# Moves, loads and sums of a fused attention, expert and GLU kernel in another order

## The chip, the cores and the metric

The kernel runs on one core of one Trainium2 chip. The metric is device time in microseconds (us), the median of several executions of the whole program. The program computes in fp32 throughout, with most products written as three fp32r products of high and low parts.

## The reference

Three parts follow one another. Attention: every query attends only to the keys that fall into its bucket of a random projection. Then each token goes to the one of eight experts with the largest logit and is weighted by its gate. Last comes RMS normalisation and a gated linear unit (GLU).

```python
# q, k, v: (2, 8, 768, 64); proj: (64, 6)
q_bits = einsum('bhsd,dk->bhsk', q, proj) > 0        # k_bits likewise
q_bucket = sum(q_bits * 2 ** arange(6), -1)
mask = q_bucket[:, :, :, None] == k_bucket[:, :, None, :]
scores = where(mask, q @ k^T / 8, -1e9)
attn = exp(scores - max(scores)); attn /= sum(attn) + 1e-9
x = (attn @ v) as (1536 tokens, 512)
# experts: w_gate (512, 8), w1 (8, 512, 1024), w2 (8, 1024, 512)
logits = x @ w_gate; e = argmax(logits); gate = softmax(logits)[e]
x = gate * (max(x @ w1[e], 0) @ w2[e])
# GLU: w_gate, w_val (512, 1536), w_out (1536, 512)
xn = x / sqrt(mean(x * x) + 1e-6) * rms_g
g = xn @ w_gate
out = (g * sigmoid(g) * (xn @ w_val)) @ w_out
```

## The kernel before

**Engines and queues.** The order of the work is written out by hand (`manual_schedule`): each engine takes its instructions in the order in which the program emits them, and nearly all DMAs are issued by SP's queue, in that order too. A DMA in that queue that waits for its source holds back all that come after it.

**Attention.** There are 16 heads (two batches of eight), with 768 tokens in six tiles of 128. The loop at line 931 runs over 96 units, one for each head and query tile; `n` is the head of unit `u` and `t` its tile. In each unit a string of letters (`ORDER`, in the last four units `LATE`) fixes the order of the steps: scores of the unit after next ("S"), maxima, exponentials of the next unit, transposes of the exponentials, the product with v ("A", `av`), the handing back of a finished group of three tiles (`keep`, `give_back`), and one step of a filler ("f", `fill_next`). A filler is a generator; the one that matters here is `prep_head(n)`, in eight steps: PE transposes k and q of the head (line 514), ACT and DVE write their scaled high and low parts `kqh` and `kql` (lines 516, 517), PE multiplies with the projection (lines 544 to 546), and DVE and POOL make of the signs the feature rows `ft` (lines 551, 552). In between, `moves()` (line 508) places the parts with six DMAs from SBUF to SBUF into qA, qB, kA and kB, the operands of the scores (lines 563, 564), and two more DMAs (lines 554, 555) bring `ft` there. `kqh`, `kql` and `ft` have one buffer each, so the next head's are written only when these moves have read them. `ML` says for which heads the moves go out already with the second cast (heads below ML) and not behind the first projection.

`load_head(n)` issues the loads of k, q and (from head 2 on) v. Before the loop the program emits, in this order: the loads of heads 0 and 1, the preparation of head 0, four steps of head 1's preparation, the loads of v of heads 0 and 1 and of the gate weights `wd`, the splitting of v of head 0 by POOL (`split_v`, lines 479 and 480), the loads of head 2 and of the RMS weights `rg`, the first scores, and the other four steps of head 1. The preparation of head 2 is put in at the end of unit 2, so its first step, the transposes, comes at the end of unit 3, just ahead of the scores of unit 6, the first of head 1.

`fill_windows(e)` writes the padding value into the 256 rows of expert e's window of the DRAM buffer `xs`, by two DMAs of 257 KB; it runs at the third and sixth unit of heads 1 to 4, two experts a head. The tokens are scattered over it later.

**Handover to the experts.** Each group of three tiles is handed back by products with an identity that has the gate weights beside it (line 667), so that the tokens by features and the head's share of the eight logits come out together in PSUM. ACT copies them to SBUF as `tb` (line 680), POOL scales the logits by the inverse sum and adds them to `LG`, and scales the features into `X` (lines 693 to 696). The last group (g = 31) comes as three single tiles with a copy each (line 685), and DVE scales and adds its logits. Then `route` chooses the expert (lines 726 to 736), PE counts ranks (line 753), and DVE makes a one-hot `hot` for each of the last three tiles (line 802). The first expert's window is not read back from DRAM alone: it is summed in PSUM (`xacc`) from products of `hot` with the last three tiles (`add_hot`, line 873) and from the window loaded as `base` (`add_base`, line 842: two products with the identity for each of four chunks). While PE waits for the routing, it runs warm-up matmuls (lines 385 and 1023). A branch (line 1044) on the number of overflowing tokens, which every engine loads from `total` (line 1042), jumps over a part that is not run with these inputs.

**Experts.** For each of eight experts: four blocks f of the first product (lines 1222 to 1224, 24 matmuls each), then four of the second (lines 1251 to 1253). The weights come in pieces through a ring of buffers and are split by ACT and DVE. `finish_rows` gates the result, normalises it and scatters it to DRAM (`yd`); it is a generator, and `next(done)` takes one of its steps after each block of the next expert's first product. Its third step holds the reciprocal, both scalings (line 205) and both scatters, and the load of window e + 3 follows it. `fill_pe` takes one step of a list of fillers on PE, such as the transposes of the next window (line 1180).

**GLU.** `flip_y` transposes the twelve tiles of results (line 1141) that `load_y` brings from `yd` (line 1130). Three tiles are loaded after the first block of the last expert, the others one by one as the three buffers come free (`YB`). The flips start after the fourth block of the last expert's first product; five run there, three in the first `glu` and four in the first `project`.

## Time and profile before

| | us |
|---|---|
| median of three runs | 735.92 (735.87 to 736.73) |
| profiled execution | 735.27 |
| its span, first to last instruction | 733.6 |
| attention, up to the warm-up at the handover | 0 to 256 |
| first product of the first expert | 264.7 |
| first flip of the results | 429.2 |
| last matmul | 726.3 |

The profile is of one execution. PE is the matmul engine (PEld its weight loads), DVE the vector engine, ACT the scalar engine, POOL GpSimd and SP the engine that issues DMAs. Times in a timeline are counted from the start of the span. What stands in brackets is how long the engine was idle before an instruction, and which event ended that by the profile; where an instruction waits for several things, the profile names the one whose event came last, and it can be wrong.

### The profile page before, as it was taken

How to read it: one execution, taken by the hardware profiler on the slowest of the kernel's cores; microseconds unless marked ns; L12 is line 12 of the kernel's file. 1: busy time of each engine (PE TensorE's matmuls, PEld its weight loads, DVE VectorE, ACT ScalarE, POOL GpSimd, SP SyncE). 2: the span in 40 equal slices, each digit the busy share in tenths (PEclk: the TensorE clock that was granted, in tenths of full speed). 3: DMA queues.
4: the chain of work that ended last, by engine and by line, in shares of the span. 5: the costliest groups of instructions: out<-in, count | busy, mean ns of one | idle time of the engine just before them, and what ended most of it. 6: DMA issues, size and time to landing. Idle time of an engine off the chain costs nothing.

```text
span 733.6 us, 12489 instructions
## 1 busy us (share of the span) xinstructions
PE 717.4 (98%) x4451; PEld 651.7 (89%) x4452; DVE 577.8 (79%) x1095; ACT 402.9 (55%) x805; POOL 225.6 (31%) x405
## 2 busy tenths in 40 slices
PE   8899999999999999999999999999999999999996
PEld 7798999999999889999999988888888888888885
DVE  6899999999999757787688777756777778778533
ACT  5798998998998735667665555533211222212210
POOL 5143344446635520213022313211211212211124
PEclk9999999999999999999999999999999999999999
DMA  7699856556742147677788674221221121200013
GB/s 182 163 254 263 213 152 154 139 147 173 190 109 70 45 146 246 197 222 246 249 264 265 218 250 150 97 87 58 61 84 58 57 87 59 86 29 1 0 58 115
DMA packets 80546, 103.44 MB, mean 141 GB/s; under 512 B 31799, under 2 KB 50231, under 8 KB 80480
## 3 DMA queue, kind: packets, MB, share of 16 engines
q1 hardware_dynamic: 76480, 92.95, 44.4%
q0 software_dynamic: 3200, 9.46, 3.5%
q8 instruction: 36, 0.59, 0.4%
q10 hardware_dynamic: 800, 0.20, 0.1%
q14 instruction: 30, 0.25, 0.1%
HBM read 69.53 MB, written 14.72 MB: 115 GB/s over the span
## 4 chain that ended last, share of the span: by engine, by line
PE 56%; issue 2%; POOL 2%; ACT 1%; DVE 1%; DMA 1%; SPq 0%; POOLq 0%; DVEq 0%
PE pg L1292 4%; PE pv L1293 4%; PE pg L1293 4%; PE pg L1291 4%; PE pv L1291 4%; PE pv L1292 4%; PE ph L1222 4%; PE ph L1223 4%; PE ph L1224 4%; PE py L1251 3%; PE py L1253 3%; PE py L1252 3%; PE z L1319 3%; PE z L1317 3%; PE z L1318 3%
## 5 line engine op out<-in xcount | busy, mean ns | idle before, releaser
L330 POOL TENSOR_TENSOR wa<-wa,hi 128x512 f32<-128x512 f32 x36 | 58.4, 1623 | 235.4 <-ACT hi L326 203.6
L326 ACT CAST hi<-wa 128x512 fp32r<-128x512 f32 x36 | 22.4, 621 | 151.3 <-DVE wa L324 147.2
L582 ACT ACTIVATE P<-S,negm 128x768 f32<-128x768 f32 x96 | 95.8, 998 | 10.5 <-DVE negm L573 6.4
L611 DVE TENSOR_TENSOR ptl<-T,pth 128x384 fp32r<-128x384 f32 x192 | 97.3, 547 | 1.5 <-ACT pth L610 0.8
L568 DVE TENSOR_REDUCE neg<-S 128x1 f32<-128x768 f32 x96 | 90.8, 946 | 3.6 <-PE S L564 2.9
L610 ACT CAST pth<-T 128x384 fp32r<-128x384 f32 x192 | 83.3, 488 | 3.6 <-PE T L601 2.9
L601 PE MATMUL T<-ident,P 128*128 128x128 f32 x576 | 81.8, 275 | 1.0 <-DVE ptl L611 0.5
L601 PEld LDWEIGHTS T<-ident,P 128*128 128x128 f32 x576 | 67.5, 141 | 7.8 <-DVE ptl L611 4.2
L285 DVE TENSOR_TENSOR lo<-raw,hi 128x1024 fp32r<-128x1024 f32 x58 | 68.7, 1216 | 4.6 <-ACT hi L284 4.6
L284 ACT CAST hi<-raw 128x1024 fp32r<-128x1024 f32 x58 | 60.2, 1055 | 21.0 <-DMA raw<-in_moe_w_dram 20.6
L563 PE MATMUL S<-kA,qA 76*128 76x384 f32 x192 | 66.2, 345 | 3.8 <-ACT kqh L516 1.8
L564 PE MATMUL S<-kB,qB 128*128 128x384 f32 x192 | 63.1, 329 | 0.4 <-DMA qB<-kql 0.4
L1222 PE MATMUL ph<-xTh,hi 128*128 128x256 f32 x224 | 62.6, 279 | 0.0
L1223 PE MATMUL ph<-xTl,hi 128*128 128x256 f32 x224 | 61.6, 275 | 0.0
L1224 PE MATMUL ph<-xTh,lo 128*128 128x256 f32 x224 | 61.6, 275 | 0.0
L633 PE MATMUL O<-ptl,vst 128*64 128x384 f32 (+1 forms) x198 | 59.8, 332 | 0.0
L1317 PE MATMUL z<-hi,hi 128*128 128x512 f32 x144 | 54.9, 381 | 0.0
L1291 PE MATMUL pg<-gxh,hi 128*128 128x512 f32 x144 | 54.7, 380 | 0.0
L1291 PE MATMUL pv<-gxh,hi 128*128 128x512 f32 x144 | 54.7, 380 | 0.0
L1292 PE MATMUL pg<-gxl,hi 128*128 128x512 f32 x144 | 54.7, 380 | 0.0
L1293 PE MATMUL pg<-gxh,lo 128*128 128x512 f32 x144 | 54.6, 379 | 0.0
L1292 PE MATMUL pv<-gxl,hi 128*128 128x512 f32 x144 | 54.6, 379 | 0.0
(236 smaller groups left out, 1911.8 us busy)
## 6 DMA issues: line engine op xcount, KB each, us to landing
raw<-in_moe_w_dram SPq DMA_DIRECT2D x64, 512.0 KB
raw<-in_moe_w_gate_dram SPq DMA_DIRECT2D x12, 512.0 KB
raw<-in_moe_w_val_dram SPq DMA_DIRECT2D x12, 512.0 KB
raw<-in_moe_w_out_dram SPq DMA_DIRECT2D x12, 512.0 KB
xs<-fill SPq DMA_DIRECT2D x16, 257.0 KB
xw<-xs SPq DMA_DIRECT2D x7, 514.0 KB
yt<-yd SPq DMA_DIRECT2D x12, 256.5 KB
qA<-kqh SPq DMA_DIRECT2D x16, 192.0 KB
```

The source lines that it names most:

```text
L568: nc.vector.tensor_reduce(neg[u % 4][:, 1:2], St[u][:, :, 0:HW], AX.XY, ALU.max, negate=True)
L582: nc.scalar.activation(p_, St.pop(u)[:, :, 0:HW], AF.Exp, bias=nm[:, 1:2], scale=nm[:, 0:1], accum_out=sums[n][:, t:t + 1])
L601: nc.tensor.transpose(w[:, c * P:(c + 1) * P], p_[:, j, c * P:(c + 1) * P], ident)
L610: nc.scalar.copy(hi[:, 3 * j:3 * j + 3, cs], wv)
L611: nc.vector.tensor_tensor(lo[:, 3 * j:3 * j + 3, cs], wv, hi[:, 3 * j:3 * j + 3, cs].bitcast(F32), ALU.subtract)
L1222: nc.tensor.matmul(ph[:, s_], wh[:, c, fs], turns(xh[:, c]), start=c == 0, stop=False)
L1223: nc.tensor.matmul(ph[:, s_], wh[:, c, fs], turns(xl[:, c]), start=False, stop=False)
L1224: nc.tensor.matmul(ph[:, s_], wl[:, c, fs], turns(xh[:, c]), start=False, stop=c == KC - 1)
L1291: nc.tensor.matmul(ps_, wh[:, c, fs], turns(xTh[b][:, c]), start=c == 0, stop=False)
L1292: nc.tensor.matmul(ps_, wh[:, c, fs], turns(xTl[b][:, c]), start=False, stop=False)
L1293: nc.tensor.matmul(ps_, wl[:, c, fs], turns(xTh[b][:, c]), start=False, stop=c == KC - 1)
L1317: nc.tensor.matmul(z, hi[:, s_, ts_], turns(oh_[:, s_]), start=s_ == 0, stop=False)
```

## The change

The moves of head 1 go out with its second cast (ML = 2), ahead of the loads of v and `wd`. The loads of head 2 follow the last four steps of head 1, and the RMS weights are loaded in head 10. The fills of the windows run in heads 6 to 9 instead of 1 to 4 (FN = 6). The single tiles of the last group write their logits and features straight from PSUM, and those of the group before it take their logits from PSUM by DVE. The two single tiles after the first share one buffer of another pool. The sums with the identity become transposes that accumulate. The register load for the branch stands ahead of the last sums. `finish_rows` has a further step before each scaling, and `next(done)` is called in the second product too. Five tiles of results are loaded at once, two of them into a window buffer; the flips start one block earlier, and their places in `glu` and `project` change.

```diff
-ML = 1
+ML = 2
+FN = 6
+    YX = 2
@@ finish_rows
         for j in range(J):
+            yield
             nc.vector.scalar_tensor_tensor(y[:, j, 0:DM], y[:, j, 0:DM], st[:, 6, j:j + 1], rg, ALU.mult, ALU.mult)
@@ keep
-                if t0 == 1:
-                    o = ld.tile([P, T, 2 * D], F32, tag="kq", name="osbl")[:, 0]
+                if tn == 1 and t0 > 0:
+                    if t0 == 1:
+                        spare.append(ld.tile([P, T, 2 * D], F32, tag="kq", name="osbl"))
+                    o = spare[-1][:, t0]
@@ give_back, single tiles
-                if t0 == 0:
-                    spare.append(sp.tile([P, 3, PE], F32, tag="tb", name=f"tb{g}"))
-                tb = spare[1]
-                nc.scalar.copy(tb[:, t0], w[:, 0:PE])
+                ls = LG[b][:, 3 * j + t0]
+                r = rinv[n][:, 1, 3 * j + t0:3 * j + t0 + 1]
+                nc.vector.scalar_tensor_tensor(ls, w[:, D:PE], r, ls, ALU.mult, ALU.add)
+                nc.scalar.activation(X[b, j][:, t0, h * D:(h + 1) * D], w[:, 0:D], AF.Copy, scale=r)
                 if t0 < 2:
                     return
@@ give_back, groups of three
-            eng = nc.vector if n == NH - 1 and j == 1 else nc.gpsimd
+                lv, eng = tb[:, :, D:PE], nc.gpsimd
+                if g == 2 * NH - 2:
+                    lv, eng = w[:, 0:3 * PE].rearrange("p (t a) -> p t a", a=PE)[:, :, D:PE], nc.vector
@@ add_base
-                nc.tensor.matmul(xacc[c][:, j * P:(j + 1) * P], base[0][:, j, cs], ident, start=False, stop=j == 1)
+                nc.tensor.matmul(xacc[c][:, j * P:(j + 1) * P], base[0][:, j, cs], ident, start=False, stop=j == 1,
+                                 is_transpose=True)
@@ before the loop
         split_v(0)
         cgen = constants()
-        load_head(2)
-        nc.sync.dma_start(rg, moe2_rms_g.partition_broadcast(P))
 ...
         for i in range(WARM[6]):
             next(fills[0])
+        load_head(2)
@@ in the loop
-            if t in (2, 5) and n > 0 and 2 * (n - 1) + t // 3 < E:
-                fill_windows(2 * (n - 1) + t // 3)
+            if t in (2, 5) and 0 <= 2 * (n - FN) + t // 3 < E:
+                fill_windows(2 * (n - FN) + t // 3)
+            if u == 10 * T:
+                nc.sync.dma_start(rg, moe2_rms_g.partition_broadcast(P))
@@ handover
         add_hot(1, range(KC))
+        any_over = nc.values_load(total[0:1, 0:1], min_val=0, max_val=N)
         for c in range(KC):
 ...
-    any_over = nc.values_load(total[0:1, 0:1], min_val=0, max_val=N)
@@ flip_y
-            if tt + YB < end:
+            if tt >= YX and tt + YB < end:
                 load_y(tt + YB)
@@ experts
-                    for tt in range(YB):
-                        load_y(tt)
-                if e == E - 1 and f == NF - 1:
+                    early = mp.tile([P, 2, XC], F32, tag="xw", name="ytx", bufs=3)
+                    for tt in range(YX + YB):
+                        load_y(tt, early[:, tt, 0:DM + 1] if tt < YX else None)
+                if e == E - 1 and f == 2:
                     fillers.append(flips)
@@ second product of an expert
                 parts.pop(i)
+                next(done, None)
                 fill_pe()
@@ glu and project
-        steps = 3
+        steps = 2
 ...
+                    if p_ == 0 and b == 1 and s_ == 1:
+                        next(flips)
 ...
-                if p_ + b == 0:
+                if p_ + b == 0 and i % 2:
                     next(flips)
```

## Rows read from the trace of the kernel before

**Rows 1.** The page: busy time, share of the span, instructions

```profile
PE 717.4 (98%) x4451; PEld 651.7 (89%) x4452; DVE 577.8 (79%) x1095; ACT 402.9 (55%) x805; POOL 225.6 (31%) x405
```

**Rows 2.** PE's waits: waited for, us in total, times, longest

```profile
PE S L563 <- ACT kqh L516: 1.8, 1, 1.8
...
PE S L563 <- DMA kA<-ft: 1.1, 1, 1.1
...
PE f L1141 <- DMA yt<-yd: 0.9, 1, 0.9
PE wk L753 <- DVE oh L735: 0.7, 1, 0.7
...
PE ph L1222 <- PEq L1044: 0.4, 1, 0.4
```

**Rows 3.** PE's timeline at head 1's first scores: start, duration, instruction, idle before

```profile
22.13 0.49 PE L514 MATMUL wf<-evens,kq 128*128 128x128 f32 x3
24.43 0.40 PE L563 MATMUL S<-kA,qA 76*128 76x384 f32 x1 [1.81 <-ACT kqh L516]
```

**Rows 4.** Timeline of SP's queue at the start

```profile
7.89 1.12 SPq L361 DMA_DIRECT2D v<-in_v_dram  x2
...
17.16 0.67 SPq L508 DMA_DIRECT2D qB<-kqh  x1
...
18.94 0.75 SPq L555 DMA_DIRECT2D kA<-ft  x1
```

**Rows 5.** Timeline of DVE at the start

```profile
10.56 1.14 DVE L517 SCALAR_TENSOR_TENSOR kql<-wf,scv,kqh 128x384 fp32r<-128x384 f32 x2 [1.29 <-DMA qB<-kql]
```

**Rows 6.** Timeline of POOL at the start

```profile
11.02 0.52 POOL L479 TENSOR_SCALAR vst<-v 128x384 fp32r<-128x384 f32 x1 [2.17 <-DMA v<-in_v_dram]
11.62 1.02 POOL L480 TENSOR_TENSOR vst<-v,vst 128x384 fp32r<-128x384 f32 x1
14.43 1.08 POOL L552 TENSOR_SCALAR ft<-ft 12x384 fp32r<-12x384 f32 x2 [1.79 <-DVE ft L551]
```

**Rows 7.** PE's timeline: its last matmul, and warm-up matmuls at the start

```profile
726.31 0.38 PE L1319 MATMUL z<-hi,lo 128*128 128x512 f32 x1
...
1.41 2.31 PE L385 MATMUL warm<-ones 128*128 128x128 bf16 x20 [1.41 <-DVE ones L372]
...
5.16 1.06 PE L385 MATMUL warm<-ones 128*128 128x128 bf16 x8
...
9.32 0.61 PE L385 MATMUL warm<-ones 128*128 128x128 bf16 x8
```

**Rows 8.** Windows: length, busy PE, PEld, DVE, ACT, POOL, clock, DMA share, GB/s

```profile
730.00:731.00 1.00, 0.00 (x0) 0.00 (x0) 0.00 (x0) 0.00 (x0) 0.00 (x0) 0.53 0.46 176
```

**Rows 9.** Windows of 20 us in attention, same columns

```profile
60.00:80.00 20.00, 18.94 (x137) 17.67 (x137) 18.80 (x38) 17.01 (x38) 8.52 (x20) 1.00 0.95 246
...
120.00:140.00 20.00, 20.00 (x144) 18.55 (x144) 19.65 (x43) 17.79 (x40) 9.92 (x22) 1.00 0.52 125
```

**Rows 10.** Timeline of DVE at the handover to the experts

```profile
257.10 0.18 DVE L726 TENSOR_REDUCE rst<-LG 128x3 f32<-128x24 f32 x1
```

**Rows 11.** PE's timeline at the handover

```profile
251.75 0.84 PE L601 MATMUL T<-ident,P 128*128 128x128 f32 x6
...
256.03 1.50 PE L385 MATMUL warm<-ones 128*128 128x128 bf16 x24
...
261.73 0.60 PE L842 MATMUL xacc<-ident,xw 128*128 128x128 f32 x4
262.09 0.48 PE L873 MATMUL xacc<-hot,ftx 128*128 128x256 f32 x2
```

**Rows 12.** The chain that ended last, at the last expert: start, us, what

```profile
433.05 6.14 DMA yt<-yd
```

**Rows 13.** PE's timeline in the last expert: its first matmul, the first flip

```profile
418.49 0.27 PE L1222 MATMUL ph<-xTh,hi 128*128 128x256 f32 x1
...
429.21 0.60 PE L1141 MATMUL f<-ident,yt 128*128 128x128 f32 x4
```

More of the change, by code (lines that the diff above doesn't have):

```diff
@@ L681, in give_back @@
             else:
-                if t0 == 0:
-                    spare.append(sp.tile([P, 3, PE], F32, tag="tb", name=f"tb{g}"))
-                tb = spare[1]
-                nc.scalar.copy(tb[:, t0], w[:, 0:PE])
+                ls = LG[b][:, 3 * j + t0]
+                r = rinv[n][:, 1, 3 * j + t0:3 * j + t0 + 1]
+                nc.vector.scalar_tensor_tensor(ls, w[:, D:PE], r, ls, ALU.mult, ALU.add)
+                nc.scalar.activation(X[b, j][:, t0, h * D:(h + 1) * D], w[:, 0:D], AF.Copy, scale=r)
                 if t0 < 2:
                     return
-            lv = tb[:, :, D:PE]
             scale = rinv[n][:, 1, 3 * j:3 * j + 3].unsqueeze(2)
-            lg = sp.tile([P, 3, E], F32, tag="lg", name=f"lg{g}")
-            eng = nc.vector if n == NH - 1 and j == 1 else nc.gpsimd
-            ls = LG[b][:, 3 * j:3 * j + 3]
-            eng.tensor_tensor(ls if h == 0 else lg, lv, scale.to_broadcast([P, 3, E]), ALU.mult)
-            if h > 0:
-                eng.tensor_tensor(ls, lg, ls, ALU.add)
-            nc.gpsimd.tensor_tensor(X[b, j][:, :, h * D:(h + 1) * D], tb[:, :, 0:D], scale.to_broadcast([P, 3, D]),
-                                    ALU.mult)
+            if tn == 3:
+                lg = sp.tile([P, 3, E], F32, tag="lg", name=f"lg{g}")
+                ls = LG[b][:, 3 * j:3 * j + 3]
+                lv, eng = tb[:, :, D:PE], nc.gpsimd
+                if g == 2 * NH - 2:
+                    lv, eng = w[:, 0:3 * PE].rearrange("p (t a) -> p t a", a=PE)[:, :, D:PE], nc.vector
+                eng.tensor_tensor(ls if h == 0 else lg, lv, scale.to_broadcast([P, 3, E]), ALU.mult)
+                if h > 0:
+                    eng.tensor_tensor(ls, lg, ls, ALU.add)
+                nc.gpsimd.tensor_tensor(X[b, j][:, :, h * D:(h + 1) * D], tb[:, :, 0:D], scale.to_broadcast([P, 3, D]),
+                                        ALU.mult)
             if h == H - 1 and (b == B - 1 or j == 1):
@@ L1126, in lsh_attention_moe_glu, with load_y @@
     yt = {}
-    def load_y(tt):
-        t = gx.tile([P, DM + 1], F32, tag="yt", name=f"yt{tt}", bufs=YB)
+    def load_y(tt, t=None):
+        if t is None:
+            t = gx.tile([P, DM + 1], F32, tag="yt", name=f"yt{tt}", bufs=YB)
         ins = nc.sync.dma_start(t, yd[tt * P:(tt + 1) * P, :]).ins
```

## The prediction

> **What bounds the kernel now.** I read the page first: TensorE is busy for 98% of the span [rows 1], so the time is PE's work plus the little that PE idles. The second view is therefore the list of PE's waits. It is short: 1.8 us at the scores of head 1, 1.1 at the scores of head 4, 0.7 and 0.4 where attention hands over to the experts, 0.9 where the last expert hands over to the GLU [rows 2]. No more than about 5 us can be gained there, and the change works at each of these places. Third, for each place, the timelines of the engines that release it.
>
> One label misleads. The scores of head 1 start at 24.43 and are put down to ACT's cast kqh [rows 2, 3]. They don't read that cast (it is of head 2). They read qA and kA of head 1, whose last piece (kA<-ft) SP issues at 18.94 [rows 4]; a DMA that is 5.5 us from issue to use, behind everything queued before it, explains the time better. So the start is a chain through SP's queue, and that queue is what the change reorders. Of the rows at 22.13 and 24.43 the reader is to see this: PE takes its instructions in order, the flips of head 2 (wf, line 514) stand just ahead of those scores, and had no wait, since kq of head 2 had been loaded long before.
>
> **Part by part. First, the start.** SP's order becomes: three moves of head 0, six moves of head 1, v of heads 0 and 1, the gate weights, the two ft moves of head 1, and only then k, q, v of head 2. Now v of head 0 is issued at 7.89, ahead of the moves [rows 4]; the six moves go later. Who then waits for whom:
> - Moves 2 to 6 of head 1 read kql, which DVE finishes at 10.56 + 1.14 = 11.70 [rows 5]; the step that writes it doesn't move. Five issues at 0.67 each, the row of the last move [rows 4]: v of head 0 goes out at 11.70 + 3.35 = 15.05 instead of 7.89.
> - From its issue to POOL's use, v took 11.02 - 7.89 = 3.1 us with three moves ahead on the rings [rows 4, 6]. With six ahead it is more; the crowded case is the 5.5 us of kA<-ft. Bounds 3.1 and 5.5. I take 4.3, since k, q and v of head 2 and the RMS weights no longer stand in front: POOL can split v at 19.35.
> - POOL's queue is in order, and the scaling of ft stands behind that split. Split 0.60 + 1.02, ft 1.08 [rows 6]: ft is ready at 22.05 (now 15.5).
> - SP then issues the two ft moves, 2 x 0.8 [rows 4], then k of head 2 (0.67) and q at 24.3. At the 3.1 us of v, q lands at 27.4.
> - PE reaches the flips of head 2 at 22.13 as now (the split of v is in time for the first output product, or nearly), and stands there until 27.4. Now the scores follow the flips after 24.43 - 1.81 - 22.13 = 0.5 us [rows 3], so they start at 27.9, and not at 24.43: **3.5 us lost**. Bounds by v's landing: 2.3 and 4.7. What was meant to go, the 1.8 us, is inside this: the moves are early, but they were not what ended last; ft and kq of head 2 are.
>
> Behind the waiting ft moves in SP's queue stand the loads of heads 2 and 3. Head 3 is wanted a head later, so only head 2 counts.
>
> **The clock** is a second charge on the same stall. PE's last matmul ends at 726.31 + 0.38 = 726.7, and the window 730 to 731 has a mean granted clock of 0.53 [rows 7, 8]. So the clock left its upper level (2.4 GHz) for the lower (1.2) at about 730.06, when PE had been idle for 3.4 us. The stall here is 27.4 - 22.1 = 5.3 us. The way back shows at the start: 20 matmuls of 128 columns from 1.41 took 2.31 us, and the eight at 5.16 still took 1.06, against 0.61 for the eight at 9.32 [rows 7]. So until about 6.2, nearly 5 us after the first matmul, the lower level held, and half of such a stretch, 2.4 us, is lost. Bounds 0 and 2.5; I take **2.2 us**. The Trainium skill, in "TensorE: Matmul & The Clock Gate", section "HAM oscillation — how this bites in real kernels", speaks against the change here: a DMA wait between bursts of matmuls sends the clock to its lower level and the next burst starts cold. By that rule the charge comes with the stall. The end of this trace agrees: the clock fell when PE stood idle.
>
> **Fills and RMS weights later.** Sixteen fills of 257 KB leave heads 1 to 4 for heads 6 to 9. From 60 to 80 us the DMA engines are busy for 0.95 of the time at 246 GB/s [rows 9], and that is where head 4's scores wait 1.1 us for kA<-ft [rows 2]. Without the fills that wait goes: 1.1 us gained. Where the fills go, 120 to 140 us, the share is 0.52 at 125 GB/s [rows 9]; four fills of 257 KB in a head of about 15 us (16 heads in some 240 us) add some 70 GB/s, and no wait of PE stands there now. I cost them at nothing. If this cover is gone, the price is one wait like the present one, 1.1 us a head.
>
> **Last logits from PSUM.** ACT's copies of the last tiles and DVE's product and sum fall away from the path to the routing's first reduction at 257.10 [rows 10]; one DVE operation on PSUM a tile replaces them, and the ACT copy of the third tile no longer waits for a buffer. From the end of PE's products (256.0, where the warm-up matmuls start [rows 11]) to 257.10 there is 1.1 us; I leave 0.4 of it for the one operation. That gives 0.7, which is also the wait that PE has [rows 2]; more can't be had, as the warm-up matmuls end at 256.03 + 1.50 = 257.53.
>
> **Sums by transposes.** Each of four chunks has two products with the identity, which PE holds as four records in 262.09 - 261.73 = 0.36 us [rows 11]. A transpose is one record (six for six flips [rows 11]) and not two. Half is saved: 4 x 0.18 = 0.7. But what ends last behind it is the branch, on which PE waits 0.4 [rows 2]; its register load moves ahead of the last sums, so a part goes too. And the first of these sums needs a window read back from DRAM, which no row shows landing. Together the handover could give from 0.4 to 1.8; I take **0.9**, the middle, as the window's load doesn't move with the routing.
>
> **Results loaded five at once, flips earlier.** The 0.9 us wait is for a load of yt that took 6.1 us [rows 12], issued only when a buffer came free. With five at once it goes. But the first flip is now wanted one block earlier. It stands at 429.21, the expert starts at 418.49, so a block is 2.7 us, and it is wanted at 426.5 [rows 13]. The loads go out after the first block, 421.2; at 6.1 us the first lands at 427.3. A new wait of up to 0.8, at least 0. I take 0.4: **0.5 gained**.
>
> **Smaller RMS steps** hold DVE and ACT for shorter pieces, and put the next expert's window load two steps later. PE has no wait in the experts [rows 2]; cost nothing. If the window came too late, PE would stand at its flips.
>
> **Sum**, against the profiled execution (735.27 us, its span 733.6): + 3.5 + 2.2 - 1.1 - 0.9 - 0.5 = + 3.2, so 738.5. The median of the runs is 735.92, 0.65 above that execution: **739.1**.
>
> **Rivals.**
> - The clock stays up, because the stall is shorter (its lower bound, 2.3 us of loss, leaves 4.1 us of idle) or something keeps it up. Without the 2.2 us the time is 736.9; at the lower bound of the stall 735.7. For it: the trace has one such fall only. Against: at either bound PE stands idle for longer than it did before that fall. Chance 0.22.
> - The start is not worse, and the change is faster. The mechanism is the landing of q of head 2: if it lands by the time at which scores of head 1 start now, about 24, nothing is lost and the 2.5 us of the other parts stay: 733.4; if the scores start at 22.6, without any wait, it gives another 1.8: 731.6. It decides from scores at 25.5. That needs v split on POOL some 3 us earlier than I have it, so v landing about 1 us after its issue, or a queue that isn't in the program's order. Against: the 3.1 us of v and the in-order rows of POOL and SP. For: rings that are nearly empty at 10 to 13 us. Chance 0.21.
> - On top of the forecast a new wait elsewhere: fills against moves in heads 6 to 9 (1.1 a head), or the first flip at its upper bound. 741 to 743. Chance 0.07.
>
> **How the numbers follow.** The forecast has 0.50. The range goes from 732.5 (it takes in most of the faster case) to 742.0 (the upper bounds of stall and clock, 739.1 + 1.2 + 0.3, and a new wait of 1.1). About 0.2% (1.5 us) can be told from no change. Slower (over 737.4): the forecast, the last rival and a little of the first, 0.58. Within: most of the first rival, 0.2. Faster (under 734.4): 0.22. The likeliest case's own range is 737 to 741.
>
> **What would show it.** PE's timeline between 20 and 30 us: right, if PE stands at the flips of head 2 and the scores of head 1 start near 28, with POOL's split of v at about 19 and the clock down behind the stall. Wrong, if the flips have no wait. No wait at the scores of head 4; the reduction of the last logits at 256.4 on the old scale; line 842 in half its time; no wait at the fourth flip and a short one at the first. If the time is under 734, the chain from v over POOL and ft to kq of head 2 is what I misjudged.

## The result, and the profile after

The changed kernel takes 744.77 us (median of six runs, 742.03 to 746.42) against 735.89 for the kernel before: a ratio of 1.0117, with a 95% interval from 1.0098 to 1.0136. So it is slower, by 8.9 us. Its profiled execution took 742.65 us, with a span of 741.0.

The first table to make from two traces is the shift of the same instruction along the way. Times are PE's, in us from the start of the span:

| | before | after | shift |
|---|---|---|---|
| first scores of head 1 | 24.43 | 27.84 | +3.41 |
| first scores of head 2 | 39.68 | 45.60 | +5.92 |
| first scores of head 3 | 54.54 | 60.45 | +5.91 |
| first scores of head 4 | 70.73 | 75.34 | +4.61 |
| last rank product (wk) | 258.24 | 263.14 | +4.90 |
| first expert product | 264.74 | 268.87 | +4.13 |
| end of the last expert's products | 442.54 | 449.32 | +6.78 |
| last matmul | 726.31 | 733.11 | +6.80 |
| end of the span | 733.56 | 740.97 | +7.40 |

Two losses (+5.9 by head 2, +2.65 in the experts) stand against two gains of about 1.3 and 0.8. The page alone hides this: PE is busy for 97% of the span, where it was 98% [rows 1], and the clock's row has an 8 in two of forty slices where it had only nines.

```profile
PE 719.4 (97%) x4443; PEld 653.6 (88%) x4444; DVE 579.3 (78%) x1098; ACT 402.8 (54%) x805; POOL 234.7 (32%) x402
...
PEclk9899999999999999999999999999999999999998
```

PE's waits (what was waited for, us in total, times, longest) name both losses. These lines answer [rows 2]: the waits at the scores of heads 1 and 4 are gone, one of 4.7 and one of 2.9 us have come.

```profile
PE wf L517 <- DMA kq<-in_q_dram: 4.7, 1, 4.7
PE f L1152 <- DMA ytx<-yd: 2.9, 1, 2.9
...
PE wk L761 <- DVE oh L743: 0.9, 1, 0.9
PE ph L1233 <- PEq L1054: 0.5, 1, 0.5
```

**The start.** PE's timeline, answering [rows 3]:

```profile
27.32 0.87 PE L517 MATMUL wf<-evens,kq 128*128 128x128 f32 x3 [4.75 <-DMA kq<-in_q_dram]
27.84 0.67 PE L566 MATMUL S<-kA,qA 76*128 76x384 f32 x1
```

SP's queue, answering [rows 4]: v now goes out at 15.54 (it was 7.89), the last ft move at 21.70 (18.94), and only behind it q of head 2.

```profile
15.54 1.18 SPq L364 DMA_DIRECT2D v<-in_v_dram  x2
...
21.70 0.78 SPq L558 DMA_DIRECT2D kA<-ft  x1
...
23.24 0.64 SPq L353 DMA_DIRECT2D kq<-in_q_dram  x1
```

POOL's timeline, answering [rows 6], gives the reason for the late ft move: POOL stands idle for 10.22 us until v has landed, and the scaling of ft stands behind the split of v.

```profile
18.89 0.52 POOL L482 TENSOR_SCALAR vst<-v 128x384 fp32r<-128x384 f32 x1 [10.22 <-DMA v<-in_v_dram]
19.49 1.02 POOL L483 TENSOR_TENSOR vst<-v,vst 128x384 fp32r<-128x384 f32 x1
20.59 1.08 POOL L555 TENSOR_SCALAR ft<-ft 12x384 fp32r<-12x384 f32 x2
```

**The clock.** Windows of the trace (length, then busy us of PE, PEld, DVE, ACT, POOL, then granted clock, DMA share, GB/s) show what the stall brings: from 28 to 33 us the granted clock is 0.50, that is the lower level of 1.2 GHz, while PE works without a pause. The two windows after them answer [rows 9]: with the fills moved, the DMA share falls from 0.95 to 0.63 in head 4's stretch, and rises from 0.52 to 0.78 where the fills now run.

```profile
22.00:26.00 4.00, 0.57 (x4) 0.24 (x2) 1.49 (x5) 0.45 (x2) 2.38 (x7) 1.00 0.50 117
...
28.00:33.00 5.00, 5.00 (x21) 4.64 (x20) 2.99 (x7) 2.80 (x6) 0.33 (x2) 0.50 0.15 41
...
60.00:80.00 20.00, 20.00 (x148) 18.84 (x147) 19.69 (x42) 18.51 (x42) 7.72 (x18) 1.00 0.63 155
120.00:140.00 20.00, 20.00 (x148) 18.82 (x147) 19.72 (x43) 18.38 (x41) 7.70 (x18) 1.00 0.78 205
```

**The handover.** DVE's timeline, answering [rows 10]. The first reduction comes at 261.94, 4.84 later than before, which is the shift that the whole stage has: nothing is gained ahead of it. Two operations of the group before (`lg`, and its sum) stand in front of those on the last three tiles.

```profile
260.70 0.18 DVE L701 TENSOR_TENSOR lg<-wo,rinv 128x24 f32<-128x24 f32 x1 [2.05 <-ACT tb L685]
260.92 0.38 DVE L703 TENSOR_TENSOR LG<-lg,LG 128x24 f32<-128x24 f32 x1
261.41 0.23 DVE L690 SCALAR_TENSOR_TENSOR LG<-spare,rinv,LG 128x8 f32<-128x8 f32 x1
261.55 0.35 DVE L690 SCALAR_TENSOR_TENSOR LG<-wo,rinv,LG 128x8 f32<-128x8 f32 x2
261.94 0.18 DVE L734 TENSOR_REDUCE rst<-LG 128x3 f32<-128x24 f32 x1
```

PE's timeline there, answering [rows 11]: two records a chunk instead of four, and chunks 0.45 us apart (266.66 to 267.12).

```profile
266.66 0.38 PE L850 MATMUL xacc<-ident,xw 128*128 128x128 f32 x2
...
267.12 0.38 PE L850 MATMUL xacc<-ident,xw 128*128 128x128 f32 x2
...
268.87 0.38 PE L1233 MATMUL ph<-xfhi,hi 128*128 128x256 f32 x1 [0.46 <-PEq L1054]
```

**The last expert.** PE's timeline, answering [rows 13], then POOL's:

```profile
433.87 0.66 PE L1152 MATMUL f<-ident,ytx 128*128 128x128 f32 x4 [2.87 <-DMA ytx<-yd]
```

```profile
417.97 1.23 POOL L170 DMA_INDIRECT yd<-y,posw  x1 [13.98 <-ACT hi L287]
...
419.75 4.63 POOL L170 DMA_INDIRECT yd<-y,posw  x1 [0.44 <-DMA raw<-in_moe_w_dram]
```

Before, the second of these two scatters stood at

```profile
412.56 1.14 POOL L168 DMA_INDIRECT yd<-y,posw  x1 [0.20 <-issue]
```

SP issues the loads of the results (`ytx`) at 430.27. By the chain that ended last (start, us, what) it waits for the second scatter, which lands at 430.20:

```profile
419.75 10.45 DMA yd<-y,posw
...
430.27 3.55 DMA ytx<-yd
```

The scatters wait for the two scalings of the normalisation, and between these DVE now does a weight split:

```profile
416.44 0.74 DVE L208 SCALAR_TENSOR_TENSOR y<-y,yst,rg 128x512 f32<-128x512 f32 x1
417.10 1.22 DVE L288 TENSOR_TENSOR lo<-raw,hi 128x1024 fp32r<-128x1024 f32 x1
418.23 0.75 DVE L208 SCALAR_TENSOR_TENSOR y<-y,yst,rg 128x512 f32<-128x512 f32 x1
```

### The profile page after: what moved, and what is told of

It is laid out like the page before. It is cut to its first block, busy times and chain, and to the rows that moved or that the text cites. A ratio compares the mean times of both kernels' runs of the same rounds, so it can differ in the third digit from the quotient of the medians.

```text
span 741.0 us, 12465 instructions
## 1 busy us (share of the span) xinstructions
PE 719.4 (97%) x4443; PEld 653.6 (88%) x4444; DVE 579.3 (78%) x1098; ACT 402.8 (54%) x805; POOL 234.7 (32%) x402
## 4 chain that ended last, share of the span: by engine, by line
PE 48%; DVE 5%; issue 3%; DMA 3%; ACT 2%; POOL 2%; POOLq 0%; DVEq 0%; ACTq 0%; SPq 0%
PE pg L1305 4%; PE pv L1304 3%; PE pg L1304 3%; PE pv L1306 3%; PE pv L1305 3%; PE pg L1306 3%; PE z L1332 3%; PE z L1333 3%; PE z L1334 3%; PE ph L1233 3%; PE ph L1235 3%; PE ph L1234 3%; PE py L1263 3%; PE py L1265 3%; PE py L1264 3%
## 5 line engine op out<-in xcount | busy, mean ns | idle before, releaser
L170 POOL DMA_INDIRECT yd<-y,posw x16 | 35.3, 2207 | 105.2 <-ACT hi L287 68.5
```

## The experiments

The theory from these rows: the early moves at the start and the smaller RMS steps each cost several us, and everything else in the change is worth a gain. The rivals: that another part brings the loss at the start or in the experts, that the clock carries most of it, or that the runs differ for another reason. Three of the first five kernels make a square of the two suspects with the changed one, then the parts that are left are undone one by one.

**The start undone.** The changed kernel with the order of the loads at the start as before (the RMS weights stay late):

```diff
-ML = 2
+ML = 1
         cgen = constants()
+        load_head(2)
 ...
             next(fills[0])
-        load_head(2)
```

> The changed kernel with the start of the kernel before (ML = 1, loads of head 2 ahead of the first scores; the RMS weights stay late). Theory (the chain v, POOL's split, ft, loads of head 2 makes the stall, and the stall makes the clock fall): the flips of head 2 have no wait, the scores of head 1 start at 24.2 or somewhat earlier (the RMS weights no longer in the queue), the clock stays at its upper level until the end, and the 5.9 us that head 2 was late go: 742.65 - 5.9 = 736.8. Rival (the fills or something behind them hold the start or the clock): the time stays above 741.

Measured: 736.23 us, ratio to before 1.0017 (1.0002 to 1.0033); the changed kernel is 8.5 us above that. No wait at the flips of head 2, the scores of head 1 start at 22.81, and the clock stays up. That is 1.6 us earlier than before; at the start this kernel differs from that of before only in the RMS weights, which are no longer in front of the moves. The wait at the first flip is still there:

```profile
PE f L1152 <- DMA ytx<-yd: 3.0, 1, 3.0
```

So the start costs most of the loss (by the ratios 1.00 of 1.17%), and the wait in the experts stands without it.

**The start alone.** The kernel before with `ML = 2`, `load_head(2)` behind the steps of head 1 and the RMS weights in head 10:

```diff
-ML = 1
+ML = 2
-        load_head(2)
-        nc.sync.dma_start(rg, moe2_rms_g.partition_broadcast(P))
 ...
             next(fills[0])
+        load_head(2)
```

> The kernel before with the start of the changed one alone (ML = 2, loads of head 2 behind ft, RMS weights in head 10); fills as before. Theory: the same stall of 4.7 us at the flips of head 2 and the same fall of the clock, so head 2 some 5.9 us late; less than that at the end if the wait at head 4 (1.1) is shortened. 735.9 + 5 to 6 = 741 to 742, no wait of flips at the last expert beyond 0.9. Rival (several parts of the change add up to the loss at the start): under 738.

Measured: 742.62 us, ratio 1.0108 (1.008 to 1.0135). The start alone is enough for most of the loss. Its wait is longer than in the changed kernel, and head 4 still waits, as the fills are still there:

```profile
PE wf L514 <- DMA kq<-in_q_dram: 5.7, 1, 5.7
...
PE S L563 <- DMA kA<-ft: 1.3, 1, 1.3
```

**The stall filled with matmuls.** The changed kernel with 78 warm-up matmuls ahead of the flips of head 2, so that PE is late but not idle:

```diff
+                if n == 2 and j == 0:
+                    keep_warm(78, ps_w, "w")
```

> The changed kernel with 78 warm-up matmuls (128 columns, some 0.056 us each, 4.4 us) on PE ahead of the flips of head 2. Theory: the stall stays (flips at 27.3), but the clock does not fall, so head 2 is 3.4 us late and not 5.9: 742.65 - 2.5 = 740.1, and the runs lie closer together than the changed kernel's 742 to 746.4. Rival (the slow stretch after the stall is not the clock but latencies of ACT and DVE, or the spread has another cause): head 2 still 5.9 us late, or the same spread.

Measured: 742.75 us, ratio 1.0111 (1.0084 to 1.0137). Windows at the start and at the handover, same columns as above:

```profile
20.00:40.00 20.00, 18.40 (x175) 16.85 (x174) 14.39 (x34) 11.65 (x27) 7.70 (x21) 1.00 0.62 151
260.00:275.00 15.00, 11.84 (x98) 11.41 (x98) 7.16 (x28) 3.76 (x8) 4.72 (x8) 0.89 0.40 123
```

The clock stays at 1.00 at the start, where the changed kernel has 0.83 in the same 20 us. From the scores of head 1 (28.66) to those of head 2 (43.84) it takes 15.18 us, as before (15.25), and not 17.76 as in the changed kernel. That is the clock's charge there: 2.5 us. But this kernel's profile has its fall elsewhere, 0.89 over 15 us at the handover, behind a wait of 1.91 us at the branch that is 0.46 in the changed kernel. The wait takes back 1.45 us and the fall 1.4 (the first expert lasts 23.66 us instead of 22.22):

```profile
268.12 0.35 PE L1235 MATMUL ph<-xfhi,hi 128*128 128x256 f32 x1 [1.91 <-PEq L1056]
```

The branch instruction itself lasts 3.70 us on PE's queue here, and 0.37 or 0.46 us in each of the other profiles; why was not found. The clock's charge at the start is shown; that it can be had back by keeping PE busy isn't, since here it was lost again: the expected 740.1 us did not come.

**The RMS steps undone.** The changed kernel without the further step of `finish_rows` and without its call in the second product:

```diff
         for j in range(J):
-            yield
 ...
                 parts.pop(i)
-                next(done, None)
                 fill_pe()
```

> The changed kernel without the smaller RMS steps (no step between the scalings, none taken in the second product). Theory (the second scatter of expert 5 comes late, and SP holds the load of the results until it has landed): SP issues the first load of results at about 426 on the changed kernel's scale and not at 430.3, and the first flip waits 0.8 us at most instead of 2.9: 2.1 to 2.9 us less than the changed kernel. Rival (the flip waits because it is one block earlier and five loads crowd each other): the wait stays above 2 us, the time is the same.

Measured: 741.7 us (740.86 to 742.53), ratio 1.0089 (1.0064 to 1.0114): 3.1 us less than the changed kernel, though its wait at the start was longer in the profile (5.5 us). The first flip waits 0.6 us instead of 2.9:

```profile
PE f L1151 <- DMA ytx<-yd: 0.6, 1, 0.6
```

**Both undone.** The two edits together.

> The changed kernel with both the start and the RMS steps of the kernel before; fills and RMS weights late, logits from PSUM, transposing sums, five loads at once and flips one block earlier stay. Theory (the loss has two places, start and second scatter): scores of head 1 at 22.8, first expert's product 3.0 us earlier than in the kernel before (261.7), first flip waits 0.6; end of the experts 2.5 to 3 us earlier than before: 732 to 733.5, faster than the kernel before by 0.2 to 0.4%. Rival (something else in the last expert eats it): 735 or more.

Measured: 732.08 us (731.27 to 733.2), ratio 0.9947 (0.9928 to 0.9966), faster than both kernels by more than the intervals. The square, in us:

| | RMS steps as before | RMS steps smaller |
|---|---|---|
| start as before | 732.08 | 736.23 |
| start changed | 741.70 | 744.77 |

The start costs 9.6 and 8.5 us, the RMS steps 4.2 and 3.1. By the ratios to the kernel before on the same chip it is 10.4 and 7.4 us, and 5.2 and 2.1 (1% is 7.36 us). So the start costs something whether the RMS steps are there or not. For the RMS steps that holds by the medians only with the start as before: the intervals of the two kernels in the lower row overlap, and there the traces have to show it. From the first expert product to the last matmul the profiles have 464.24 us (changed kernel) and 462.81 (RMS steps undone), and 464.82 and 462.82 with the start as before. That is 1.4 and 2.0 us. What the medians have above that is not in these profiles. The rest of the change is worth 3.5 us against the kernel before (735.55 beside it). Behind the first warm-up matmuls PE's waits are short (0.6 at the first flip); the longest:

```profile
PE S L565 <- ACT P L584: 0.9, 4, 0.4
PE wk L760 <- DVE oh L742: 0.9, 1, 0.9
```

The last expert's first product lasts 12.31 us in this profile and 14.59 in the changed kernel's: 2.3 us for the flip wait. Some of it comes back elsewhere: from the first expert product to the start of the last expert it is 154.46 us here and 153.94 in the changed kernel.

**Which link of the start.** As the last, but with the moves of head 1 early and v of heads 0 and 1 loaded ahead of them. If the late v is the cause, this has the early moves without the loss:

```diff
-ML = 1
+ML = 2
+        load_v(0)
+        load_v(1)
 ...
-        load_v(0)
-        load_v(1)
-        load_head(2)
 ...
             next(fills[0])
+        load_head(2)
```

> The changed kernel's start (ML = 2, loads of head 2 behind ft), but with the loads of v of heads 0 and 1 issued ahead of the moves of head 1; RMS steps as before. It tests the link v to POOL: theory: v lands at 11, POOL splits it then, ft is scaled at 14.4 and moved by SP at 15.5 to 17, loads of head 2 land by 21, no wait at the flips (22.1), scores of head 1 at 22.6 to 22.9, no fall of the clock, time as with the whole old start, 732 to 733.5. Rival (the loads of head 2 are late because they stand behind the moves and ft, whatever v does): the flips wait 2 us or more, time over 735.

Measured: 733.81 us, ratio 0.9971 (0.9955 to 0.9987). POOL splits v at 11.01 and scales ft at 14.42, as the kernel before did, and most of the loss is gone. The late v is thus the main link. The flips still wait, which was not expected: q of head 2 stands behind the moves.

```profile
23.36 0.52 PE L516 MATMUL wf<-evens,kq 128*128 128x128 f32 x3 [1.08 <-DMA kq<-in_q_dram]
23.64 0.41 PE L565 MATMUL S<-kA,qA 76*128 76x384 f32 x1
```

The scores start at 23.64, against 22.45 with the start as before (the fifth kernel; 21.91 to 23.91 in the six profiles that have this start), and the time is 1.7 us above the fifth kernel's. Early moves gain nothing even with v in time.

**The logits undone.** The fifth kernel with the copies and sums of the last logits as before:

```diff
-                ls = LG[b][:, 3 * j + t0]
-                r = rinv[n][:, 1, 3 * j + t0:3 * j + t0 + 1]
-                nc.vector.scalar_tensor_tensor(ls, w[:, D:PE], r, ls, ALU.mult, ALU.add)
-                nc.scalar.activation(X[b, j][:, t0, h * D:(h + 1) * D], w[:, 0:D], AF.Copy, scale=r)
+                if t0 == 0:
+                    spare.append(sp.tile([P, 3, PE], F32, tag="tb", name=f"tb{g}"))
+                tb = spare[1]
+                nc.scalar.copy(tb[:, t0], w[:, 0:PE])
...
-                if g == 2 * NH - 2:
-                    lv, eng = w[:, 0:3 * PE].rearrange("p (t a) -> p t a", a=PE)[:, :, D:PE], nc.vector
+            eng = nc.vector if n == NH - 1 and j == 1 else nc.gpsimd
```

> The kernel with both the start and the RMS steps of before, and in addition the last logits as before (copies by ACT, product and sum). Theory (three single operations and the group before them now stand in a row on DVE, so the routing's first reduction comes no earlier): the count of ranks (wk) comes at the same time after the warm-up matmuls within 0.2 us, same total time. Rival (logits from PSUM do save, and something else ate it): wk 0.5 us later or more.

Measured: 732.4 us, ratio 0.9951 (0.9934 to 0.9968), the same as the fifth kernel within the intervals. In the traces, from the first scores of head 15 to the first reduction it is 22.67 us with logits from PSUM and 22.74 with the old path. They bring nothing that can be seen.

**The transposes undone.** The fifth kernel with plain products in `add_base`:

```diff
-                nc.tensor.matmul(xacc[c][:, j * P:(j + 1) * P], base[0][:, j, cs], ident, start=False, stop=j == 1,
-                                 is_transpose=True)
+                nc.tensor.matmul(xacc[c][:, j * P:(j + 1) * P], base[0][:, j, cs], ident, start=False, stop=j == 1)
```

> The kernel with the start and the RMS steps of before (732.08 us), with the base set added by plain products instead of transposes. By the theory that the transposes carry the whole gain of the handover, the chunks of the sums come every 0.68 us instead of every 0.455, the first expert product comes 0.8 us later behind the first base product (3.0 us instead of 2.2), and the time is 732.9 (732.5 to 733.3). By the rival that the handover's gain is that of the branch value read earlier, the first expert product stays where it is and the time is 732.1.

Measured: 734.0 us, ratio 0.9975 (0.9961 to 0.9989). From the first sum at the identity to the first expert product it takes 2.95 us (258.59 to 261.54), with transposes 2.21 (259.00 to 261.21): 0.74 us, as the first theory says. The kernel before, without the earlier register load, has 3.01 (261.73 to 264.74), so that load brings 0.1 at most. The median lies 1.9 above the fifth kernel's and outside what was expected; the profile has a first flip that waits 1.56 us instead of 0.57, which would be the rest of it. Whether that is chance or follows from the sums was not settled.

**The flips undone,** still with five loads at once:

```diff
-                if e == E - 1 and f == 2:
+                if e == E - 1 and f == NF - 1:
                     fillers.append(flips)
 ...
-        steps = 2
+        steps = 3
```

> The kernel with both the start and the RMS steps of before, and the flips at their old places (after the fourth block, three in the first glu, four in the first project); five loads at once stay. Theory (the earlier flip brings the wait, the five loads alone remove the old one): no wait at any flip of the last expert, from the first product of the first expert to the first of the GLU 177.1 us instead of 178.0 before, about 0.6 us less than with the early flips. Rival (five loads land too late as well): a flip still waits 0.5 us or more.

Measured: 732.94 us, ratio 0.9961 (0.9945 to 0.9978). No flip of the last expert waits, as the theory says, but the 0.6 us that this was to bring did not come. A flip in the first `glu` now waits 1.09 us (1.15 in the next kernel) until DVE has split an earlier tile, and on DVE the last expert's scalings stand ahead of that split. In the kernel before, that flip has no such wait. PE's timeline, then DVE's:

```profile
449.40 0.65 PE L1151 MATMUL f<-ident,yt 128*128 128x128 f32 x4 [1.09 <-DVE gxl L1157]
```

```profile
447.33 1.42 DVE L207 SCALAR_TENSOR_TENSOR y<-y,yst,rg 128x512 f32<-128x512 f32 x2
```

**Flips and logits undone together.** The edits of the last experiment and of that on the logits in one kernel, again on the fifth:

```diff
-                if e == E - 1 and f == 2:
+                if e == E - 1 and f == NF - 1:
...
-                nc.vector.scalar_tensor_tensor(ls, w[:, D:PE], r, ls, ALU.mult, ALU.add)
+                nc.scalar.copy(tb[:, t0], w[:, 0:PE])
```

> The kernel with the start and the RMS steps of before (732.08 us), and also with the flips, the five loads and the last logits as before: what is left of the change is the late RMS weights, the late fills, the transposes and the branch value. By the theory that the logits bring nothing and the flips with the five loads little, 732.9 us (732.3 to 733.5). If both gained what the prediction gave them (0.7 and 0.9), 733.7.

The expectation says that the five loads are as before too; they are not, this kernel still issues five at once. Measured: 732.8 us, ratio 0.9965 (0.9951 to 0.998). The intervals of the last two overlap with that of the fifth kernel. From the first expert product to the last matmul the profiles have 462.82 us (fifth kernel), 462.84 (old flips), 461.82 (old flips and logits) and 461.57 (before). So earlier flips and logits from PSUM gain nothing that can be seen, and by elimination nearly all of the 3.5 us is left to the late RMS weights, the late fills and the transposes. For the fills the traces agree: from the scores of head 3 to those of head 4 it is 16.2 and 16.4 us in the two kernels with the early fills, and 14.9 in all others. Five loads by themselves were not tried.

**The changed kernel, profiled twice more.** Its median lies 2.1 us above its profiled execution. Two more profiles of the same program:

> The changed kernel as it is, profiled again: its other five runs (742.0 to 746.4 us, median clock 0.990) lie above the one that was profiled (742.65, clock 0.992). By the theory that the difference is one more fall of TensorE's clock behind a wait, a profile at 744 us or more shows a third fall beside that at the start and that of the last 6 us, most likely behind the 2.9 us wait for the first flip (434 us) or the handover's (about 269 us), worth 1.5 to 3 us; a profile near 742.5 shows none. By the rival, that the slower runs wait longer for a transfer, there is no third fall and a wait is longer by 2 us.

> The changed kernel as it is, a third profile. So far: 742.65 us with a fall of the clock of 6.83 us at the start, 740.35 us with one of 3.41 us, both with the same wait of 4.7 to 4.8 us. By the theory that the runs differ by the number of such stretches at the lower level, a run near 744 to 746 us has another 3.41 us or more of it, at the start or behind a later wait, and one at 740 or 742.5 us repeats the two seen. By the rival, runs differ by the waits for transfers alone, and the falls don't go with the time.

Measured: 740.35 and 744.15 us. Windows at the start and at the first flip, first of the profile at 742.65, then of that at 740.35, then of that at 744.15:

```profile
20.00:40.00 20.00, 14.64 (x85) 13.33 (x84) 12.48 (x30) 10.61 (x23) 6.42 (x20) 0.83 0.49 121
...
430.00:440.00 10.00, 7.13 (x54) 6.65 (x53) 7.26 (x15) 4.72 (x11) 0.00 (x0) 1.00 0.79 263
```

```profile
20.00:40.00 20.00, 14.78 (x93) 13.35 (x92) 13.56 (x32) 11.24 (x25) 6.74 (x20) 0.91 0.55 138
...
430.00:440.00 10.00, 8.02 (x55) 7.49 (x56) 6.95 (x14) 4.73 (x11) 1.61 (x3) 1.00 0.86 291
```

```profile
20.00:40.00 20.00, 14.28 (x89) 12.83 (x88) 12.89 (x30) 10.98 (x25) 6.75 (x20) 0.83 0.51 126
...
430.00:440.00 10.00, 6.93 (x46) 6.69 (x45) 5.31 (x12) 4.37 (x10) 0.00 (x0) 0.83 0.72 244
```

The clock is the last column but two. The slowest profile has a further fall behind the first flip (0.83 over 10 us): from that flip to the end of the experts it takes 17.08 us, against 15.45 in the other two, so this fall costs 1.6 us. That is the largest item in its 3.8 us above the fastest one; of the others, 0.6 is a longer wait at the start, 0.6 a longer wait at the flip, 0.6 comes between the scores of heads 13 and 14. The profile at 742.65 is 2.3 above the fastest: 1.1 between the scores of heads 1 and 2 (17.76 against 16.67 us), where the clock was down for longer, 0.6 in the tail, 0.4 at the flip. In the profile at 744.15 the mean at the start is 0.83 too, but the fall came earlier, while PE still waited (0.59 from 24 to 28 us, 0.83 in the first profile), and from the scores of head 1 to those of head 2 it takes 16.76. So the clock is the largest single item in both differences, but under half of each; longer waits and stretches without a known cause make up the rest.

## Why the prediction was wrong

It said slower, and named the right chain at the start; it was 5.7 us short, and 744.77 lies above the 742.0 at which its range ends. The step that failed is the cost of the flips and the smaller RMS steps, put at a gain of 0.5 us together; then comes the distance from a profile to the median. By its steps:

**The start was right in its chain.** Flips at 27.4 and scores at 27.9 were forecast, 27.32 and 27.84 came; v at 15.54 (forecast 15.05), POOL's split at 18.89 (19.35), ft ready at 21.67 (22.05). The stall of +3.5 was +3.41. That the sum came to 0.1 us is luck in part: v took 3.35 us from issue to POOL where 4.3 was taken, and q of head 2 took 4.1 where 3.1 was taken. One of the two ft moves had gone out at 18.21, ahead of the scaled ft, so q was issued at 23.24 and not at 24.3. And only the second and third of the six moves read kql; the others stand behind them. The kernel with v ahead shows that the late v was the main link.

The reading of before was right too: the scores of head 1 did not wait for the cast that the label named [rows 2, 3]; in the fifth kernel they start at 22.45, and that cast only at 22.71. They waited for the moves; that it was kA<-ft is not shown (one profile names qA<-ft). With the RMS weights out of SP's queue the wait is gone in three of six profiles with the start as before, and 0.4, 0.5 and 1.2 us in the others; the scores start at 21.91 to 23.91, where the one profile of before has 24.43. The rival "start not worse" had that scores at 22.6 without a wait would give 731.6 us; the kernel that has it, with the RMS steps undone as well, takes 732.08. The gain existed, but it came from the late RMS weights, and the early moves gave it away.

**The clock was right in size and incomplete.** 2.2 us were taken. From the scores of head 1 to those of head 2 the three profiles lose 2.5, 1.4 and 1.5 us against before's 15.25. The kernel with the stall filled shows that it is the clock. The Trainium skill's rule that a DMA wait leaves the next burst of matmuls cold ("TensorE: Matmul & The Clock Gate", section "HAM oscillation — how this bites in real kernels") agrees with this trace: 0.50 from 28 to 33 us. What the sum lacked is that a shorter new wait can bring the charge too: behind the first flip it cost 1.6 us in one profile of three, and that profile (744.15) is the one near the median. It does not come with every wait: behind 2.5 and 2.9 us at that flip there was none. The rival "the clock stays up" is out: the clock fell in all three.

**Fills: right.** 1.1 forecast; the shift falls by 1.30 between heads 3 and 4. The fills' new place was forecast 70 GB/s busier and is 80 (125 to 205), and no wait of PE stands there.

**Handover: the sum right, its parts not.** 0.9 was taken, 0.77 came (the shift falls from 4.90 to 4.13). All of it is the transposes, forecast at 0.7 and measured at 0.74. The logits, forecast at 0.7, gave nothing: the step that failed is "one DVE operation on PSUM a tile replaces them". The change also moves the product and the sum of the group before from POOL to DVE, and these stand in the same queue just ahead; five operations take 1.24 us (260.70 to 261.94), where 1.1 was the whole stretch from PE's products to the reduction. The wait for the ranks is 0.9 instead of 0.7, and that on the branch is still there.

**Flips and RMS steps: wrong, and the largest miss.** The forecast was -0.5; the shift grows by 2.65 in the experts, so 3.2 us of the miss lie here. Two terms failed, by 1.4 and 1.7 us in the profiles. The first failed step is "smaller RMS steps ... cost nothing". Its argument was that PE has no wait in the experts. But the steps don't only cut work into pieces, they let other work in between: DVE's second scaling comes 1.8 us after the first (416.44, 418.23) with a weight split between, the second scatter goes out by itself, and its issue takes 4.63 us instead of 1.14. It lands 10.4 us after its start, where before it took 6.1 (412.56 to 418.64). Counted from the start of the last expert's products, it goes out 2.9 us later than before and lands 7.2 later. The loads of the results wait for that landing, in SP's queue, and the first flip is wanted a block earlier than before. The prediction gave this flip a wait of at most 0.8, from the load's own 6.1 us; it had left out that the load waits for a scatter, which the change itself moves. Undoing the steps brought the wait to 0.6, within that bound. The third rival named this flip as the place of a new wait, at 0.07 and with the same bound.

The second is the gain of the flips. Undoing the RMS steps takes 1.4 us off the stretch from the first expert product to the last matmul (464.24 to 462.81); that is still 1.2 above before (461.57), where 0.5 less was forecast: another 1.7 us. The wait of 0.9 at the fourth flip is gone as forecast, but the last expert's first product lasts 12.31 us with the earlier flips (fifth kernel) and 11.07 before, as it holds one more flip and the wait of 0.6; and at the old places a flip in the first `glu` waits instead, 1.1 us. Both ways the end comes no earlier.

**Adding up.** To the forecast's 738.5 for a profiled execution come 3.2 for flips and RMS steps (some 1.4 of it the steps), 0.3 for the clock at the start, 0.1 for the handover, and 0.3 that the shift grows between the scores of head 4 and the ranks, less 0.1 and 0.2 for stall and fills; that is 742.1 of 742.65. Another 0.6 is in the tail: from the last matmul's start to the end of the span it is 7.86 us here, and 7.25 to 7.28 in all other profiles but one (7.60); why is open. From there to the median it is 2.1 us; the further fall of the clock gives 1.6 in the one profile that has it. That it stands behind the other slower runs too is likely (their mean clock is 0.990 or 0.991, that of the two faster ones 0.992) but was only argued.

## What to carry to other kernels

Before a DMA is issued earlier on an in-order queue, list what now goes behind it and who waits for that on other in-order queues: here six moves put v 7.6 us later, and through POOL and SP again that became an idle matmul engine. Cutting a step into smaller ones is not free when its last piece feeds a DMA that somebody waits for: price it by when that last piece lands. And ask of each new wait of a few us whether the clock falls behind it, and profile more than one execution before trusting a single one's sum.

## What of the hardware was not expected

The fall of the clock doesn't follow from the wait's length alone. The same program with waits of 4.7 and 4.8 us at the start had a mean clock of 0.83 and 0.91 over the same 20 us. A wait of 2.9 us at the first flip had no fall, one of 2.5 none, one of 3.0 (with the start as before) none, one of 3.1 did, and there the clock was still at 1.00 from 432 to 434 us, when PE was idle, and at 0.57 from 434 to 438, when it had work again:

```profile
432.00:434.00 2.00, 0.00 (x0) 0.00 (x0) 1.32 (x6) 0.68 (x2) 0.00 (x0) 1.00 0.71 215
434.00:438.00 4.00, 3.81 (x20) 3.81 (x21) 2.05 (x4) 1.72 (x3) 0.00 (x0) 0.57 0.91 292
```

The second is POOL's scatter. The sixteen scatters of results take 968 to 4629 ns in the changed kernel, and 973 to 1157 with the RMS steps as before, where the second of a pair starts 0.3 us after the end of the first (durations in ns, smallest, median and largest; first of the changed kernel, then with the steps undone):

```profile
L170 POOL DMA_INDIRECT yd<-y,posw x16: 968/1221/4629, 307.5 to 460.3; - x16
```

```profile
L170 POOL DMA_INDIRECT yd<-y,posw x16: 973/1024/1157, 306.6 to 460.1; - x16
```

In the changed kernel the second of a pair takes 4.35 to 4.63 us in five of the first six pairs, where it starts some 0.5 us after the first; in the other, where it starts 5 us after, it takes 1.20. In the kernel before and in the one with the steps undone, one copy of 4.33 us stands on POOL behind one pair, but behind the other pairs that two copies follow at once these take 0.9 and 1.2, and in the fifth kernel no copy is so long. So whether the long stretch in the scatter is the one in the copy is not shown, and what POOL does in it no row shows.
